# First weight tile fetched ahead of the attention's loads, and the tails' bias copied by DMA

## The chip, the cores and the metric

The program runs on one core of a Trainium2 chip. Five engines of that core matter here: TensorE (PE in the profile), VectorE (DVE), ScalarE (ACT), GpSimd (POOL) and SyncE (SP), whose queue issues every transfer of this kernel. The metric is device time in microseconds (us) of one execution; the median of three runs counts.

## The reference

What is computed, cut to its shape:

```python
# 1. attention, 4 batches x 8 heads, 576 positions, head dim 64, window 128
scores = where(mask, scale * q @ k.T + bias, -1e9); x = softmax(scores) @ v      # x: 2304 x 512
# 2. first layer pair
h = x @ w_in; g = relu(h) ** 2; x = g @ w_out                                    # 512 -> 2048 -> 512, float64 weights
# 3. eight experts, all on all tokens
P = exp(x @ w_gate - max); 8 times: rows and columns of P normalised
out = sum over e of P[:, e] * (relu(x @ w1[e]) @ w2[e])                          # 512 -> 1024 -> 512
```

The weights of step 2 arrive as float64, as pairs of 32-bit words. The kernel turns each into a high and a low fp32r part itself, and every large product is made of three matmuls (high x high, high x low, low x high).

## The kernel before

The work is staged. Attention and the first layer pair run interleaved over the first 600 us or so; the experts follow in an order that is written out by hand and lies outside the change. In the first part the order on each engine is made by a scheduler, from the code's order and its own estimate of when operands are ready. So a statement moved in the code can move instructions of every engine.

Four things matter at the start:

- **Attention units.** A unit is one batch, one pair of heads and one part of the sequence (the first 384 positions, or the rest). `attention_load` loads q and k, two transfers each, `attention_qk` turns them with PE (tiles `tp_k`, `tp_q`) and evicts them (`kf` on ACT, `qwhole` half on ACT and half on DVE). `attention_scores` makes a block of scores in `sc`: a matmul of the identity with `bias`, then two of q with k; DVE takes the minimum (`m`), ACT the exponential (`s`), DVE normalises. `attention_weights` turns `s` with PE (`pt`) and ACT copies it to `p`; `attention_values` multiplies with `v` into `xo`, which becomes the columns `xh`, `xl` of x.
- **Position bias.** DVE builds `bias` in eight instructions (line 150), and POOL masks each twice (lines 151, 155). `tails_ready` copies parts of it into `tbias` for the last 64 positions: eight ACT casts (line 183).
- **Weight tiles.** `fetch(i)` loads tile i (512 KB) into one of three buffers `u`; even tiles are of w_in, odd ones of w_out. `narrow` converts a tile: two ACT passes (lines 458, 460), four DVE passes (461, 462, 465, 469, the last one shown as CUSTOM_DVE_ANT_0 in the trace and as ISA in the order), an ACT rounding to the high part (471) and a DVE difference for the low part (472). The result is `a` (w_in) or `b` (w_out), stored to `d_in` or `d_out` for later chunks of tokens (line 499).
- **First layer.** Chunk 0 of x is the first 384 tokens, hence four attention units. Its first matmul, `h` (lines 119 to 121), needs all of that chunk and the first `a`.

In the code `load(0)` and `load(1)` (the q and k of the first two units) stand at line 443, far ahead of `fetch(0)` and `fetch(1)` at line 681, and the SP queue issues them in that order. A transfer whose condition isn't met holds everything behind it on that queue.

Of the kernel before, what the change touches and what calls it, by code (L numbers as in the profile page):

```python
# [23 lines left out]
def raw(ap):  # L24

    return ap.bitcast(F32)
# [3 lines left out]
def attention_moe_moe2(  # L30
# [12 lines left out]
    nc = tc.nc  # L43
    P = 128
# [7 lines left out]
    TAIL = S - FULL * P  # L52
# [95 lines left out]
    bias = ap.tile([P, H, 2 * P], F32R, name="bias")  # L148
# [10 lines left out]
    tbias = ap.tile([P, NPAIR, P + TAIL], F32R, name="tbias")  # L159
# [17 lines left out]
    def tails_ready():  # L177

        for i in range(SETS):
            nc.gpsimd.memset(qtail[i], 0.0)  # L180
        for hp in range(NPAIR):
            for j in range(2):
                nc.scalar.copy(
                    tbias[j * TAIL : (j + 1) * TAIL, hp, :], raw(bias[0:TAIL, 2 * hp + j, : P + TAIL])
                )

    def attention_load(n, b, hp, rest):

        h0 = 2 * hp
        t = {"rest": rest, "alone": b == 0 and not rest, "whole": n < WHOLE_UNITS}  # L190
        for nm, src in (("k", k), ("q", q)):
            r = t[nm] = ap.tile([P, 3, 2, D], F32, name=f"{nm}raw", tag=f"{nm}raw", bufs=2)
            r0 = 0 if not rest else EARLY - (0 if nm == "q" else P)
            r1 = FULL * P if rest else EARLY
            for j in range(2):
                nc.sync.dma_start(
                    r[:, : (r1 - r0) // P, j, :], src[b, h0 + j, r0:r1, :].rearrange("(t p) d -> p t d", p=P)
                )
            if rest:
                nc.sync.dma_start(  # L200
                    r[:TAIL, (r1 - r0) // P], src[b, h0 : h0 + 2, r1:, :].rearrange("j p d -> p j d")
                )
        return t
# [185 lines left out]
    def load(n):  # L389
        if n < len(units):  # L390
            ts[n] = attention_load(n, *units[n])
# [33 lines left out]
    def advance(n):  # L425
        for kind, m, i in steps[done[0] : n]:
            b, hp, rest = units[m]
            if kind == "q":
                if m == NPAIR:
                    tails_ready()  # L430
                attention_qk(m, ts[m])
                ts[m]["p"] = None
            elif kind == "s":
                attention_scores(hp, ts[m], i)
                if i in (1, FULL):
                    attention_v(m, ts[m])
                    load(m + 2)
            else:
                attention_weights(ts[m], i)
                attention_values(b, hp, ts[m], i)  # L440
        done[0] = max(done[0], n)

    load(0)
    load(1)


    NF1 = FF // P
    d_in = [dram.tile([P, 2, DM], F32, name=f"d_in{f}") for f in range(NF1)]
# [3 lines left out]
    def narrow(src, hi, lo):  # L452

        low, high = src[:, :, 0], src[:, :, 1]
        t = [cv.tile([P, DM], U32, name=f"cv{i}", tag=f"cv{i}", bufs=2) for i in range(4)]

        mag = t[0].bitcast(F32)
        nc.scalar.activation(mag, high.bitcast(F32), AF.Abs)

        nc.scalar.activation(t[3], low, AF.Copy, scale=2.0 ** -29)  # L460
        nc.vector.tensor_scalar(mag, mag, F64_SMALL, F64_LARGE, op0=ALU.max, op1=ALU.min)
        nc.vector.tensor_scalar(
            t[1], t[0], 3, 0x3FFFFFF8, op0=ALU.logical_shift_left, op1=ALU.bitwise_and
        )
        nc.vector.scalar_tensor_tensor(
            t[2], high, 0xC0000000, t[1], op0=ALU.bitwise_and, op1=ALU.bitwise_or
        )

        nc.vector.tensor_add(t[1], t[2], t[3])
        w = t[1].bitcast(F32)  # L470
        nc.scalar.activation(hi, w, AF.Copy)
        nc.vector.tensor_sub(lo, w, raw(hi))
# [3 lines left out]
    def fetch(i):  # L476

        if i < 2 * NF1:
            f, nm = divmod(i, 2)
            fs = slice(f * P, (f + 1) * P)  # L480
            words[i] = cv.tile([P, DM, 2], U32, name="u", tag="u", bufs=3)
            uv = words[i].rearrange("p c w -> p (c w)")
            if nm == 0:
                nc.sync.dma_start(
                    uv.rearrange("p (k f) -> p k f", k=NK),
                    w_in[:, fs].bitcast(U32).rearrange("(k p) f -> p k f", p=P),
                )
            else:
                nc.sync.dma_start(uv, w_out[fs, :].bitcast(U32))

    def moe1_load(c, f):
        out = []
        for j, (nm, dr, nb) in enumerate((("a", d_in[f], 3), ("b", d_out[f], 4))):
            hl = mp.tile([P, 2, DM], F32R, name=nm, tag=nm, bufs=nb)
            if c == 0:
                i = 2 * f + j
                fetch(i + 2)
                narrow(words.pop(i), hl[:, 0], hl[:, 1])
                nc.sync.dma_start(dr, raw(hl))
            else:  # L500
                nc.sync.dma_start(raw(hl), dr)
            hl = [hl[:, 0], hl[:, 1]]
            out.append([x.rearrange("p (k f) -> p k f", k=NK) if nm == "a" else x for x in hl])
        return out
# [174 lines left out]
    pending = []  # L679
    turns = [(c, f) for c in range(NCH) for f in range(NF1)]  # L680
    fetch(0)
    fetch(1)
    ahead = [moe1_load(0, 0), moe1_load(0, 1)]
    loaded = [2]
    for c in range(NCH):
# [16 lines left out]
        for f in range(NF1):  # L702
# [6 lines left out]
            hp, tag = (ps_mm, "mm") if c < NCH - 1 else (ps_at, "at")  # L709
# [574 lines left out]
```

## Time and profile before

| | us |
|---|---|
| median of 3 runs (2118.63 to 2123.6) | 2118.92 |
| profiled execution, its own time | 2118.78 |
| its span (first to last instruction) | 2117.0 |
| PE busy in the span | 2052.1 (97%) |
| DVE busy | 1430.3 (68%) |
| ACT busy | 958.4 (45%) |

The device time holds 1.78 us beside the span. A busy PE is not a PE at its peak, since matmuls are pipelined and their ends are modelled. The line of the page that cuts the span into 40 slices (53 us each) shows where PE is not busy: in the first slice, and a little in the third and fourth.

### The profile page before, as it was taken

To read this page: it belongs to the slowest core of one execution; us is meant where nothing else is said; L and a number is where in the kernel's file an instruction comes from. 1 tells how busy PE (TensorE), PEld (TensorE's weight loads), DVE (VectorE), ACT (ScalarE), POOL (GpSimd) and SP (SyncE) were. 2 spreads that over 40 slices of the span, in tenths; PEclk is the share of its full clock that TensorE was granted. 3 is DMA by queue.
4 is the path that set the end of the run, shared out by engine and by line. 5 is a ranking of instruction groups with operands and counts; after the bars stand their busy time and mean duration, and the time that the engine had idled before them with its cause. 6 is when DMAs were issued, how large, how long until landed. Compare 5 with 4: busy or idle time off the path is not lost.

```text
span 2117.0 us, 31449 instructions
## 1 busy us (share of the span) xinstructions
PE 2052.1 (97%) x11056; PEld 1859.8 (88%) x11056; DVE 1430.3 (68%) x2396; ACT 958.4 (45%) x1902; POOL 1032.7 (49%) x665
## 2 busy tenths in 40 slices
PE   6999999999998899999999999999999999999998
PEld 4877777777897787899998999999999999999998
DVE  7886444432327888877778676777768676777766
ACT  7775444433334444444444534444445534444343
POOL 1112212122437777888887444455456444455452
PEclk9999999999999999999999999999999999999999
DMA  7686756555667877887888977777887878777773
GB/s 213 227 253 209 230 154 178 158 181 171 210 202 265 294 264 282 307 319 288 309 313 296 319 264 260 256 253 254 266 264 260 271 264 259 256 250 258 264 262 125
DMA packets 281981, 525.43 MB, mean 248 GB/s; under 512 B 85840, under 2 KB 130016, under 8 KB 277728
## 3 DMA queue, kind: packets, MB, share of 16 engines
q1 hardware_dynamic: 281824, 523.42, 73.5%
q8 instruction: 89, 1.46, 0.3%
q14 instruction: 68, 0.56, 0.1%
HBM read 379.60 MB, written 143.73 MB: 247 GB/s over the span
## 4 chain that ended last, share of the span: by engine, by line
PE 59%; DVE 9%; ACT 2%; issue 2%; DMA 1%; POOL 1%; SPq 0%; ACTq 0%; DVEq 0%; POOLq 0%
PE y L120 9%; PE y L121 9%; PE y L119 9%; PE g L119 9%; PE g L121 9%; PE g L120 9%; DVE rl L954 1%; DVE o L922 1%; ACT rh L953 1%; DMA d_w<-w2a 1%; DVE o L920 1%; DVE s L644 1%; DVE s L642 1%; PE acc L120 1%; PE acc L121 1%
## 5 line engine op out<-in xcount | busy, mean ns | idle before, releaser
L1104 POOL TENSOR_TENSOR rb<-R,rb 128x768 fp32r<-128x768 f32 x95 | 212.7, 2239 | 334.6 <-ACT rb L1099 306.2
L1135 DVE TENSOR_TENSOR a<-y,a 128x384 f32<-128x384 f32 x434 | 239.7, 553 | 180.1 <-PE y L121 178.2
L1104 POOL TENSOR_TENSOR rt<-R,rt 128x768 fp32r<-128x768 f32 x125 | 238.9, 1924 | 146.1 <-issue 61.7
L111 POOL TENSOR_TENSOR gl<-r,gh 128x512 fp32r<-128x512 f32 (+1 forms) x80 | 97.1, 1214 | 397.7 <-ACT gh L110 379.1
L111 POOL TENSOR_TENSOR w2a<-r,w2a 128x1024 fp32r<-128x1024 f32 x64 | 155.4, 2430 | 67.5 <-ACT w2a L110 67.5
L1099 ACT ACTIVATE rt<-R 128x768 fp32r<-128x768 f32 x128 | 107.7, 841 | 148.7 <-DVE R L1086 90.2
L119 PE MATMUL g<-xt,w1o 128*128 128x384 f32 x512 | 172.7, 337 | 0.8 <-ACT u L827 0.6
L121 PE MATMUL g<-xt,w1o 128*128 128x384 f32 x512 | 172.4, 337 | 0.0
L119 PE MATMUL y<-rt,w2o 128*128 128x384 f32 x512 | 172.2, 336 | 0.1
L120 PE MATMUL g<-xt,w1o 128*128 128x384 f32 x512 | 172.2, 336 | 0.0
L121 PE MATMUL y<-rt,w2o 128*128 128x384 f32 x512 | 172.2, 336 | 0.0
L120 PE MATMUL y<-rt,w2o 128*128 128x384 f32 x512 | 172.0, 336 | 0.0
L120 PE MATMUL y<-w2a,rh 128*128 128x512 f32 x384 | 151.0, 393 | 0.2 <-POOL w2a L111 0.2
L119 PE MATMUL y<-w2a,rh 128*128 128x512 f32 x384 | 151.1, 393 | 0.0
L121 PE MATMUL y<-w2a,rl 128*128 128x512 f32 x384 | 150.1, 391 | 0.0
L1081 DVE TENSOR_TENSOR R<-R,pb 128x768 f32<-128x768 f32 x128 | 137.8, 1078 | 5.2 <-ACT R L1194 2.4
L716 DVE SCALAR_TENSOR_TENSOR r<-h,r 128x512 f32<-128x512 f32 (+1 forms) x80 | 50.9, 636 | 128.8 <-ACT r L714 128.7
L119 PE MATMUL y<-rb,w2o 128*128 128x384 f32 x384 | 129.8, 338 | 2.8 <-DVE a L1135 2.1
L120 PE MATMUL y<-rb,w2o 128*128 128x384 f32 x384 | 130.0, 339 | 2.4 <-POOL rb L1104 2.4
L121 PE MATMUL y<-rb,w2o 128*128 128x384 f32 x384 | 129.8, 338 | 0.0
L121 PE MATMUL g<-xb,w1o 128*128 128x384 f32 x384 | 129.1, 336 | 0.0
L119 PE MATMUL g<-xb,w1o 128*128 128x384 f32 x384 | 129.0, 336 | 0.0
(232 smaller groups left out, 5892.1 us busy)
## 6 DMA issues: line engine op xcount, KB each, us to landing
w1o<-d_w SPq DMA_DIRECT2D x448, 256.0 KB, 3.1
w2o<-d_w SPq DMA_DIRECT2D x224, 512.0 KB, 4.0
d_w<-w1a SPq DMA_DIRECT2D x32, 1792.0 KB, 11.6
d_w<-w2a SPq DMA_DIRECT2D x32, 1536.0 KB, 7.9
a<-d_in SPq DMA_DIRECT2D x64, 512.0 KB, 3.6
b<-d_out SPq DMA_DIRECT2D x64, 512.0 KB, 3.6
r<-in_moe_w_dram SPq DMA_DIRECT2D x64, 512.0 KB, 4.3
u<-in_moe_w_in_dram SPq DMA_DIRECT2D x16, 512.0 KB, 5.1
```

Of the source, the lines that this page charges most:

```text
L111: (eng or nc.gpsimd).tensor_sub(lo, src, raw(hi))
L119: nc.tensor.matmul(ps, lhsT=lh, rhs=rh, start=first, stop=False, **kw)
L120: nc.tensor.matmul(ps, lhsT=lh, rhs=rl, start=False, stop=False, **kw)
L121: nc.tensor.matmul(ps, lhsT=ll, rhs=rh, start=False, stop=last, **kw)
L642: nc.vector.tensor_sub(w1s[n][:, 2], w1s[n][:, 1], a11)
L644: nc.vector.tensor_sub(w1s[n][:, 0], a12, w1s[n][:, 2])
L716: nc.vector.scalar_tensor_tensor(g[:, :n], ph[:, :n], 0.0, r[:, :n], op0=ALU.max, op1=ALU.mult)
L920: nc.vector.tensor_add(acc[e][:, i], y, acc[e][:, i])
L1081: nc.vector.tensor_mul(r, r, pb[:, None, :].to_broadcast([P, 2, HALF]))
L1099: nc.scalar.activation(x[:, 0], R[m, f, h], AF.Copy)
L1104: eng.tensor_sub(x[:, 1], R[m, f, h], raw(x[:, 0]))
L1135: nc.vector.tensor_add(acc[dst][:, dt], ps[:, :HALF], acc[dst][:, dt])
```

## The change

Two edits, both in the first stage. `load(0)` and `load(1)` move to the fetches, so that the code's order is fetch, load, fetch, load; and the eight ACT casts of `tails_ready` become eight transfers on SP, of the same bytes from `bias` to `tbias`, read and written as plain fp32.

```diff
         for hp in range(NPAIR):
             for j in range(2):
-                nc.scalar.copy(
-                    tbias[j * TAIL : (j + 1) * TAIL, hp, :], raw(bias[0:TAIL, 2 * hp + j, : P + TAIL])
+                nc.sync.dma_start(
+                    raw(tbias[j * TAIL : (j + 1) * TAIL, hp, :]), raw(bias[0:TAIL, 2 * hp + j, : P + TAIL])
                 )
...
-    load(0)
-    load(1)
-
...
     fetch(0)
+    load(0)
     fetch(1)
+    load(1)
     ahead = [moe1_load(0, 0), moe1_load(0, 1)]
```

Line numbers behind line 443 fall by 3 or 4 in the changed kernel. The scheduler makes a new order out of it. On DVE, at the program's start (`cv` are the passes of `narrow`; the numbers tell tiles apart: 281 to 283 are tile 0, 297 tile 1), before:

```order
L107 TENSOR_TENSOR wgs<-wg,wgs 128x4x8
L143 CAST ident_r<-ident 128x128
L147 CAST rel<-rel_i 128x256
L150 TENSOR_SCALAR bias<-rel 128x256 x8
L461 TENSOR_SCALAR cv_281<-cv_281 128x512
L462 TENSOR_SCALAR cv_282<-cv_281 128x512
L221 TENSOR_SCALAR qwhole_170<-tp_q 64x3x128
L465 SCALAR_TENSOR_TENSOR cv_283<-u,cv_282 128x512
```

and now:

```order
L107 TENSOR_TENSOR wgs<-wg,wgs 128x4x8
L458 TENSOR_SCALAR cv_281<-cv_281 128x512
L459 TENSOR_SCALAR cv_282<-cv_281 128x512
L462 SCALAR_TENSOR_TENSOR cv_283<-u,cv_282 128x512
L466 ISA cv_282<-cv_283,cv_284 128x1024
L469 TENSOR_TENSOR a<-cv_282,a 128x512
L143 CAST ident_r<-ident 128x128
L147 CAST rel<-rel_i 128x256
L150 TENSOR_SCALAR bias<-rel 128x256 x8
L458 TENSOR_SCALAR cv_297<-cv_297 128x512
```

The whole conversion of tile 0 has moved ahead of the eight bias instructions. On DVE where the first two units end (`m_574`, `m_604` are the minima of the next two units' second blocks, `xl0_90` the low part of x from `xo_505`, the second unit's output), before and now:

```order
L299 TENSOR_REDUCE m_548<-sc_546 128x2
L299 TENSOR_REDUCE m_574<-sc_572 128x2
L321 TENSOR_SCALAR s_547<-s_547,z_549 128x128 x2
L299 TENSOR_REDUCE m_604<-sc_602 128x2
L115 TENSOR_TENSOR xl0_90<-xo_505,xh0_89 128x384
```

```order
L321 TENSOR_SCALAR s_547<-s_547,z_549 128x128 x2
L115 TENSOR_TENSOR xl0_90<-xo_505,xh0_89 128x384
L299 TENSOR_REDUCE m_574<-sc_572 128x2
L299 TENSOR_REDUCE m_604<-sc_602 128x2
```

The minima that open the next blocks now stand behind the second unit's output. On SP, where tiles 6 to 9 are fetched and unit 4 has its v loaded, before and now:

```order
L484 DMA u<-in_moe_w_in_dram 128x4x256
L266 DMA v<-in_v_dram 128x3x64 x2
L499 DMA d_in_189<-a 128x1024
L489 DMA u<-in_moe_w_out_dram 128x1024
L499 DMA d_out_211<-b 128x1024
L484 DMA u<-in_moe_w_in_dram 128x4x256
L489 DMA u<-in_moe_w_out_dram 128x1024
L263 DMA v<-in_v_dram 128x2x64
```

```order
L481 DMA u<-in_moe_w_in_dram 128x4x256
L496 DMA d_in_177<-a 128x1024
L486 DMA u<-in_moe_w_out_dram 128x1024
L496 DMA d_out_199<-b 128x1024
L183 DMA tbias<-bias 64x192 x8
L481 DMA u<-in_moe_w_in_dram 128x4x256
L486 DMA u<-in_moe_w_out_dram 128x1024
L496 DMA d_in_178<-a 128x1024
L496 DMA d_out_200<-b 128x1024
L263 DMA v<-in_v_dram 128x2x64
```

Ten transfers have come between the fetch of tile 7 and the first v load of unit 4: the eight copies, and the stores of the fourth `a` and `b`.

## Rows read from the trace of the kernel before

**Rows 1.** The page's 40 slices, busy tenths of PE and DVE.

```profile
PE   6999999999998899999999999999999999999998
DVE  7886444432327888877778676777768676777766
```

**Rows 2.** Windows: us, length, then busy us of PE, PEld, DVE, ACT, POOL, clock.

```profile
0.00:54.00 54.00, 34.42 (x182) 24.00 (x183) 41.40 (x118) 38.56 (x108) 9.24 (x29) 0.91 0.72 212
54.00:120.00 66.00, 64.95 (x382) 56.51 (x383) 58.50 (x138) 49.21 (x128) 11.82 (x13) 1.00 0.72 236
120.00:180.00 60.00, 53.42 (x296) 40.86 (x295) 54.09 (x133) 42.50 (x110) 6.87 (x7) 1.00 0.77 237
```

**Rows 3.** Timeline of the start: start us, us, engine, line, instruction [idle before].

```profile
1.23 1.03 SPq L196 DMA_DIRECT2D kraw<-in_k_dram  x2
...
3.02 0.22 DVE L143 CAST ident_r<-ident 128x128 fp32r<-128x128 f32 x1
...
3.47 2.93 DVE L150 TENSOR_SCALAR bias<-rel 128x256 fp32r<-128x256 f32 x8
...
5.49 0.49 SPq L484 DMA_DIRECT2D u<-in_moe_w_in_dram  x1
...
10.14 0.66 ACT L458 ACTIVATE cv<-u 128x512 f32<-128x512 f32 x1 [4.02 <-DMA u<-in_moe_w_in_dram]
...
10.83 0.43 DVE L461 TENSOR_SCALAR cv<-cv 128x512 f32<-128x512 f32 x1 [4.44 <-ACT cv L458]
```

**Rows 4.** Groups by line, first 60 us: busy us, mean ns | idle before.

```profile
L465 DVE SCALAR_TENSOR_TENSOR cv<-u,cv 128x512 uint32<-128x512 uint32 x9 | 6.6, 735 | 0.1
L469 DVE CUSTOM_DVE_ANT_0 cv<-cv,cv 128x1024 uint16<-128x1024 uint16 x8 | 5.5, 685 | 0.1
L461 DVE TENSOR_SCALAR cv<-cv 128x512 f32<-128x512 f32 x10 | 4.2, 420 | 5.2 <-ACT cv L458 5.2
L462 DVE TENSOR_SCALAR cv<-cv 128x512 uint32<-128x512 uint32 x9 | 3.8, 421 | 0.1
L183 ACT CAST tbias<-bias 64x192 fp32r<-64x192 f32 x8 | 2.8, 346 | 0.1
...
L471 ACT ACTIVATE a<-cv 128x512 fp32r<-128x512 f32 x4 | 2.5, 624 | 0.0
```

**Rows 5.** Timeline, DVE near 22 and 28 us.

```profile
22.05 0.69 DVE L472 TENSOR_TENSOR a<-cv,a 128x512 fp32r<-128x512 f32 x1 [1.62 <-ACT a L471]
...
27.92 0.61 DVE L321 TENSOR_SCALAR s<-s,z 128x256 f32<-128x256 f32 x2
```

**Rows 6.** Timeline from 40 us to the first layer's first matmul.

```profile
40.98 0.59 SPq L484 DMA_DIRECT2D u<-in_moe_w_in_dram  x1
...
42.14 0.47 ACT L314 ACTIVATE s<-sc,m 128x256 f32<-128x256 f32 x1 [0.63 <-DVE m L299]
...
42.60 0.48 ACT L114 ACTIVATE xh<-xo 128x384 fp32r<-128x384 f32 x1
...
45.31 0.67 ACT L458 ACTIVATE cv<-u 128x512 f32<-128x512 f32 x1 [0.38 <-DMA u<-in_moe_w_in_dram]
...
53.84 0.45 PE L119 MATMUL h<-xh,a 128*128 128x384 f32 x1
```

**Rows 7.** Timeline from 51 us: unit 4's loads, the fourth `a`, their uses.

```profile
51.51 0.38 SPq L263 DMA_DIRECT2D v<-in_v_dram  x1
...
57.30 0.36 PE L289 MATMUL sc<-tbias,ident_r 128*128 128x192 f32 x1
...
58.64 0.69 DVE L472 TENSOR_TENSOR a<-cv,a 128x512 fp32r<-128x512 f32 x1
...
60.25 0.80 SPq L200 DMA_DIRECT2D qraw<-in_q_dram  x1
...
69.55 0.47 PE L227 MATMUL tp<-ident,qraw 128*128 128x128 f32 x2
```

**Rows 8.** Transfers issued in the first 60 us: KB each, median us to landing.

```profile
qraw<-in_q_dram SPq DMA_DIRECT2D x8, 32.0 KB, 2.3
```

## Prediction

> **What bounds the kernel now.** I read the page's slices first. PE is at nine tenths or more almost everywhere; it is not in the first 53 us, and slightly less in the third and fourth slice [rows 1]. The change touches nothing behind the first stage, so I then cut the stage into windows [rows 2]. Up to 54 us PE is busy 34.42 us: 19.6 us are lost there. From 54 to 120 us it is busy 64.95 of 66 us, hence PE sets the pace. From 120 to 180 us 6.6 us are lost, with DVE busy 54.09 of 60 us; behind that PE is at nine tenths again [rows 1]. So the change can win only what brings the first matmul of the first layer, at 53.84 us [rows 6], forward, or what thins the 6.6 us later.
>
> The timeline of the start says what the 19.6 us hang on. DVE finishes the bias at 6.40 us (3.47 + 2.93) and then stands still for 4.44 us, since the first weight tile, issued at 5.49 us, is there only at 10.14 us, where ACT begins after 4.02 us of idling [rows 3]. From there to 28 us DVE stands still only once for long, 1.62 us, for an ACT rounding [rows 5]. It is DVE, then, whose queue sets when the first softmax tiles are ready.
>
> **The change, part by part.**
>
> *The tile comes earlier.* It is issued at 1.23 us instead of 5.49 us. With the same 4.65 us to landing (10.14 - 5.49) it is there at 5.88 us, and DVE starts 0.69 us behind (10.83 - 10.14), at 6.57 us [rows 3]. The time to landing is the uncertain part: the old transfer shared the engines with two more tiles, the new one with small q and k loads only. I keep 4.65 us; 1 us either way is my bound, and it shifts DVE's start by as much.
> The Trainium skill (DMA: Bandwidth & Descriptors, Anatomy of one DMA) fits a transfer issued by GpSimd as about 2.0 us fixed plus its bytes over 436 GB/s, an estimate of 3.2 us for 512 KB. The row has 4.65 us, so the measurement decides; by the page DVE would start 1.45 us earlier, and the forecast would be 2116.9.
>
> *DVE does the whole conversion before the bias.* That is the price in the new order. On DVE tile 0 takes 0.42 + 0.42 + 0.735 + 0.685 us, then waits 0.62 us for the ACT rounding [rows 4] and ends with 0.69 us [rows 5]: 3.57 us, to 10.14 us. Then come the identity, the positions and the bias, 3.38 us (3.02 to 6.40) [rows 3]: the bias is done at 13.52 us, 7.1 us later than before. POOL's masks follow the bias and move along. This delays nothing that decides: the minima on DVE stand behind the bias and four conversion passes anyway.
>
> *DVE up to 28 us.* Before, from 10.83 to 28.53 us DVE got through the third score block's normalisation, 17.70 us [rows 3, 5]. Of that 1.62 us was idle; 2.95 us was tile 0, already done now (0.42 + 0.42 + 0.735 + 0.685 + 0.69); and 0.42 us is a pass of tile 4 that now comes later. 12.71 us are left: 13.52 + 12.71 = 26.23 us. With 0.5 us of waiting for an ACT rounding I take 26.7 us, 1.8 us ahead.
>
> *The casts.* Eight of 346 ns, 2.8 us [rows 4], leave ACT between 13 and 20 us. ACT has that time free in the new order, because it waits for DVE's minima; I count them at nothing of their own. If ACT set the pace they would be worth up to 2.8 us. The copies land well before use: on SP they follow the store of the third `b`, near 44.5 us; with 0.52 us an issue (1.03 us for two [rows 3]) they are out near 48.7 us and, with the 2.3 us of a small transfer [rows 8], landed near 51 us, against a first use at 57.30 us [rows 7]. That cover is 6 us.
>
> *From 28 to 54 us.* Walking the new order with the old durations, the lead of 1.8 us holds up to the second unit's output and is then lost on ACT. The minima of the next blocks stand behind that output on DVE, so the exponentials that began at 42.14 us begin near 43.2 us. From there to the first matmul it was 11.70 us (42.14 to 53.84) [rows 6]. Two of ACT's instructions on that stretch stand elsewhere now, a conversion pass of 0.67 us and an eviction of 0.48 us [rows 6], and its 0.38 us of waiting for tile 6 goes if the tile is there: 10.2 us are left, which ends at 53.4 us. Whether the tile is there is close: its fetch of tile 6 was issued at 40.98 us and landed 4.33 us later (45.31) [rows 6]. Now v loads and q loads stand ahead of it, and it goes out near 42.5 us, lands at 46.8 us and is wanted by ACT near 47.5 us. Each microsecond beyond that would be lost in full. I take 53.4 us, 0.4 us ahead.
>
> *After 54 us.* The same matmuls, and PE paces them up to 120 us, so the 0.4 us pass through. DVE has 1.1 us more of conversion before it (a pass of 0.685 and one of 0.42 us are now behind the first matmul), against 7.5 us of idling from 54 to 120 us [rows 2]: nothing. Between 120 and 180 us the instructions shuffle a little. Nothing in the trace tells the sign; half of the 6.6 us, 3.3 us, is my bound both ways.
>
> *Sum.* 2118.78 (the profiled execution: span 2117.0 and 1.78 around it) less 0.4 = 2118.4 us. The median of the runs is 0.14 us above that execution, so nothing is added. Bounds: landing of the tile 1 us, shuffling 3.3 us, the casts 2.8 us for gains only: 2112 to 2122.5.
>
> **The rivals.**
>
> *Faster (2112).* The lead at 28 us (1.8 us) and the casts (2.8 us) both reach the first matmul, and a third of the 6.6 us goes: 6.8 us, 2112.0. For it: 19.6 us lie open at the start, and the transfer that DVE and ACT waited for comes 4.3 us sooner. Against it: the delay of the bias takes most of this back on the same queue, and ACT's path from 42 us holds no cast.
>
> *Slower (2127).* The SP queue is late for unit 4. Its v was issued at 51.51 us and its last q at 60.25 us, and PE turned that q at 69.55 us [rows 7]. Now ten more transfers stand ahead, two of them stores that wait for DVE: the fourth `a` was done at 59.33 us (58.64 + 0.69) [rows 7]. With the stores out at 60.1 us and ten loads at 0.52 us an issue [rows 3], the last q goes out near 65.3 us and is there 2.3 us later [rows 8], at 67.6 us: 1.9 us to spare. It decides from the point where that `a` slips by more than 1.9 us. At a slip of 3.9 us PE waits 2 us, and the next three units, queued behind the next stores, do the same: 8 us, 2126.8. Against it: that `a` needs only tiles fetched by 43 us.
> The Trainium skill (DMA: Bandwidth & Descriptors, Anatomy of one DMA) says that DMA engines don't wait on semaphores, the issuing sequencer does before it dispatches; the copies and stores then hold SP as this rival has it.
>
> *No effect of the first edit (2118.8).* The scheduler gives all of the lead back, and 54 us is met to the tenth. By time this is the forecast; only the trace would tell.
>
> **How the numbers follow.** Some 0.3%, 6.4 us, is what a measurement of this kernel can tell from no change, and it is larger than every single term above. The forecast with its own range of 2114 to 2122, together with the no-effect case, gets 0.80; the faster rival 0.12; the slower one 0.08. The range of 2112.5 to 2123.5 leaves out the far sides of both. Faster than 2112.5 gets 0.11, slower than 2125.3 gets 0.08, the rest 0.81.
>
> **What would show it.** In the changed kernel's timeline: ACT's first pass on tile 0 near 5.9 us, DVE's bias from about 10.5 to 13.5 us, the third block's normalisation near 26 to 27 us, tile 6 landed before ACT asks for it, and the first matmul of the first layer within 1 us of 53.4 us. In the windows PE should again be busy over 64 of 66 us behind it. The prediction is wrong if that matmul comes over 3 us from 53.84 us, if ACT waits for tile 6 with the copies of `p` behind it, if PE waits for a q or v load near 67 to 70 us, or if the idle time between 120 and 180 us changes by more than 3.3 us.

## The result, and the profile after

The changed kernel is slower: 2133.8 us (median of five runs, 2129.02 to 2134.99) against 2119.57 us (five runs, 2118.63 to 2123.6). The ratio is 1.0059 with an interval of 1.0048 to 1.007. The forecast was 2118.4 us in a range of 2112.5 to 2123.5, with 8 chances in 100 for slower. The profiled execution took 2131.24 us, with a span of 2129.4 us, 12.4 us longer than before.

First the page's slices, busy tenths in 40 equal parts of the span, which answer to [rows 1]:

```profile
PE   6989999999998999999999999999999999999998
DVE  7887444432317788887778666777668666777766
```

Only the third slice (106 to 160 us) of PE has dropped. So the windows again, which answer to [rows 2] (length, then busy us of PE, PEld, DVE, ACT, POOL, granted clock), with one of ten microseconds behind them:

```profile
0.00:54.00 54.00, 35.02 (x171) 24.61 (x172) 41.31 (x113) 34.00 (x94) 10.65 (x29) 0.91 0.68 195
54.00:120.00 66.00, 59.72 (x333) 51.08 (x332) 53.81 (x123) 43.16 (x113) 11.54 (x12) 0.97 0.65 209
120.00:180.00 60.00, 52.55 (x281) 40.00 (x279) 51.42 (x119) 40.60 (x104) 6.08 (x6) 0.97 0.76 234
100.00:110.00 10.00, 8.72 (x47) 7.81 (x48) 4.89 (x8) 3.37 (x8) 1.00 (x2) 0.83 0.85 267
```

The counts behind the x say more than the busy time, which grows when the clock falls. Up to 180 us PE has issued 785 matmuls (171 + 333 + 281) against 860 before (182 + 382 + 296). At 0.173 us each, the distance from one 128x384 matmul to the next at the full clock, the 75 that are missing are 13.0 us, about the 12.4 us of the span; this is an estimate, since not all of the 75 have that shape. Eleven of the 75 are missing by 54 us, 49 more between 54 and 120 us, 15 more up to 180 us. DVE too did less from 54 to 120 us, 123 instructions instead of 138: it was not overloaded, work reached it late.

The start went as forecast (timeline: start, length, engine, line, instruction, idle before):

```profile
1.24 0.49 SPq L481 DMA_DIRECT2D u<-in_moe_w_in_dram  x1
...
5.82 0.66 ACT L455 ACTIVATE cv<-u 128x512 f32<-128x512 f32 x1 [2.90 <-DMA u<-in_moe_w_in_dram]
6.51 0.43 DVE L458 TENSOR_SCALAR cv<-cv 128x512 f32<-128x512 f32 x1 [3.37 <-ACT cv L455]
...
9.66 0.69 DVE L469 TENSOR_TENSOR a<-cv,a 128x512 fp32r<-128x512 f32 x1 [0.70 <-ACT a L468]
...
10.72 2.92 DVE L150 TENSOR_SCALAR bias<-rel 128x256 fp32r<-128x256 f32 x8
```

SP's queue did not (start, time that the issue holds SP, count):

```profile
45.45 0.59 SPq L481 DMA_DIRECT2D u<-in_moe_w_in_dram  x1
...
48.44 6.21 SPq L183 DMA_DIRECT2D tbias<-bias  x8
54.70 0.58 SPq L481 DMA_DIRECT2D u<-in_moe_w_in_dram  x1
...
60.21 0.33 SPq L496 DMA_DIRECT2D d_in<-a  x1
61.63 0.33 SPq L496 DMA_DIRECT2D d_out<-b  x1
62.05 0.41 SPq L263 DMA_DIRECT2D v<-in_v_dram  x1
...
68.20 0.63 SPq L200 DMA_DIRECT2D qraw<-in_q_dram  x1
```

The eight copies hold SP for 6.21 us. One issue takes 0.55 us in the median; two took longer (one of them 1.02 us), and some 1.1 us lie between the issues. Behind them tile 8 goes out at 54.70 us (45.45 before), unit 4's first v at 62.05 us (51.51 [rows 7]) and its last q at 68.20 us (60.25 [rows 7]). Where the missing matmuls are felt is later, on PE:

```profile
98.10 0.33 PE L120 MATMUL acc<-gl,b 128*128 128x384 f32 x1
98.27 0.34 PE L121 MATMUL acc<-gh,b 128*128 128x384 f32 x1
98.87 0.44 PE L119 MATMUL acc<-gh,b 128*128 128x384 f32 x1 [0.26 <-ACT gh L110]
...
100.91 0.45 PE L120 MATMUL acc<-gl,b 128*128 128x384 f32 x1 [1.12 <-POOL gl L111]
101.19 0.43 PE L121 MATMUL acc<-gh,b 128*128 128x384 f32 x1
101.42 0.52 PE L119 MATMUL acc<-gh,b 128*128 128x384 f32 x1
101.74 0.52 PE L120 MATMUL acc<-gl,b 128*128 128x384 f32 x1
...
116.43 0.34 PE L121 MATMUL h<-xh,a 128*128 128x384 f32 x1
119.44 0.79 PE L119 MATMUL acc<-gh,b 128*128 128x384 f32 x3 [2.68 <-ACT gh L110]
```

Before, PE waited 0.8 us in all between 54 and 125 us: behind a group of `h` matmuls stood `acc` matmuls whose inputs were ready, or a unit's attention. Now it waits 6.6 us there, 5.1 of them for `gh` and `gl`, the high and low part of g (total us, times, longest us):

```profile
PE acc L119 <- ACT gh L110: 3.3, 3, 2.7
PE acc L120 <- POOL gl L111: 1.8, 2, 1.1
```

That reserve is used up, and PE waits for its own chain from h over r (the squared relu of h) to gh (2.68 us). After the pause at 99 us the matmuls come 0.32 us apart instead of 0.173 for some 4 us. The granted clock of 100 to 110 us is 0.83, so a part of it lies at the lower level, 1.2 GHz; from 120 to 180 us, behind the second pause, it is 0.97. Before, it was 1.00 from 54 to 180 us [rows 2].

One more thing runs out, the lead of the weights. A group of twelve `h` matmuls needs one `a`, whose conversion ends with DVE's difference for the low part. The time from that end to the group's first matmul is the lead of the conversion. In the kernel before it is 38 us at the first group and 9.6 us at the fourth. At the seventh it was 3.5 us (89.12 less 85.60); now PE meets an `a` that is not finished (92.90 less 93.56). Before:

```profile
84.91 0.69 DVE L472 TENSOR_TENSOR a<-cv,a 128x512 fp32r<-128x512 f32 x1
89.12 0.33 PE L119 MATMUL h<-xh,a 128*128 128x384 f32 x1
```

and now:

```profile
92.87 0.69 DVE L469 TENSOR_TENSOR a<-cv,a 128x512 fp32r<-128x512 f32 x1
92.90 0.33 PE L119 MATMUL h<-xh,a 128*128 128x384 f32 x1
```

In the kernel before, the lead is gone only at the ninth group, at 103 us. With both edits the lag grows from there on: the seventh group begins 3.8 us later than before, the eleventh 14.2 us, the fourteenth still 14.2 us.

### The profile page after: what moved, and what is told of

It is laid out like the page before. It is cut to its first block, busy times and chain, and to the rows that moved or that the text cites. A ratio compares the mean times of both kernels' runs of the same rounds, so it can differ in the third digit from the quotient of the medians.

```text
span 2129.4 us, 31449 instructions
## 1 busy us (share of the span) xinstructions
PE 2056.7 (97%) x11056; PEld 1862.5 (87%) x11056; DVE 1432.7 (67%) x2396; ACT 955.3 (45%) x1894; POOL 1032.9 (49%) x665
## 4 chain that ended last, share of the span: by engine, by line
PE 60%; DVE 7%; issue 2%; ACT 2%; DMA 1%; POOL 1%; SPq 0%; ACTq 0%; DVEq 0%; POOLq 0%
PE y L120 10%; PE y L121 10%; PE y L119 10%; PE g L119 9%; PE g L121 9%; PE g L120 9%; DMA d_w<-w2a 1%; DVE rl L953 1%; ACT rh L952 1%; DVE o L919 1%; DVE s L639 1%; DVE o L921 1%; PE acc L120 1%; PE acc L121 1%; PE acc L119 1%
## 5 line engine op out<-in xcount | busy, mean ns | idle before, releaser
L119 PE MATMUL acc<-gh,b 128*128 128x512 f32 (+1 forms) x320 | 128.1, 402 | 3.3 <-ACT gh L110 3.3
L121 PE MATMUL g<-xb,w1o 128*128 128x384 f32 x384 | 129.0, 336 | 0.0
## 6 DMA issues: line engine op xcount, KB each, us to landing
d_w<-w1a SPq DMA_DIRECT2D x32, 1792.0 KB, 11.4
```

The lines of the kernel that those rows point to most:

```text
L119: nc.tensor.matmul(ps, lhsT=lh, rhs=rh, start=first, stop=False, **kw)
L121: nc.tensor.matmul(ps, lhsT=ll, rhs=rh, start=False, stop=last, **kw)
```

## The experiments

Theory Q, formed from these rows: SP is held by the copies while a stage with no slack waits for what stands behind them. Rivals: the early start of edit 1 costs it (theory E); DMAs as such, or the scheduler's new order as such (theory S), cost it. All ratios are to the kernel before on the same chip. "Edit 1" is the moved fetch, "edit 2" the copies by DMA. Three columns of the table come from the traces: how long copies held SP between 43 and 55 us, from the first issue to the end of the last; DVE's instructions from 54 to 120 us (138 before); and the lead of the conversion at the seventh group of `h` matmuls (3.5 us before).

| run | SP held, us | DVE | lead, us | ratio (95% interval) |
|---|---|---|---|---|
| both edits | 6.21 | 123 | -0.7 | 1.0059 (1.0048 to 1.0070) |
| e1_fetch_only | 0 | 134 | 2.9 | 1.0012 (1.0004 to 1.0021) |
| e4_late_second | 0 | 136 | 3.5 | 1.0015 (1.0006 to 1.0024) |
| e2_dma_only | 6.45 | 123 | -0.7 | 1.0042 (1.0030 to 1.0055) |
| f7_extra8 | 6.88 | 124 | -1.2 | 1.0053 (1.0040 to 1.0066) |
| f8_no_casts | 0 | 136 | 4.4 | 1.0001 (0.9992 to 1.0010) |
| f2_two_only | 2.39 | 134 | 2.9 | 0.9997 (0.9989 to 1.0006) |
| f3_two_early | 0 | 132 | 2.0 | 1.0010 (1.0001 to 1.0019) |
| f1_two_both | 1.65 | 132 | 0.8 | 1.0028 (1.0018 to 1.0038) |
| i1_spread | 4.03 | 126 | 1.3 | 1.0021 (1.0012 to 1.0029) |
| h1_defer | 0 | 141 | 3.3 | 1.0005 (0.9997 to 1.0014) |
| h2_dma_defer | 5.43 | 126 | 1.3 | 1.0042 (1.0030 to 1.0055) |
| h4_after_defer | 7.17 | 124 | -0.7 | 1.0067 (1.0055 to 1.0080) |
| e3_pool_queue | 0 | 133 | 2.9 | 1.0026 (1.0016 to 1.0035) |
| e2_act_queue | 0 | 135 | 4.3 | 0.9998 (0.9989 to 1.0006) |
| e3_act_queue | 0 | 135 | 2.9 | 1.0008 (1.0000 to 1.0017) |
| i3_before_u4 | 0 | 141 | 9.6 | 1.0013 (1.0004 to 1.0021) |
| i2_e2_u4 | 6.74 | 133 | 7.8 | 1.0030 (1.0020 to 1.0040) |
| i4_after_u4 | 5.86 | 131 | 7.6 | 1.0060 (1.0048 to 1.0072) |

**One edit at a time.** e1_fetch_only puts ScalarE's copies back:

```diff
-                nc.sync.dma_start(raw(tbias[...]), raw(bias[...]))
+                nc.scalar.copy(tbias[...], raw(bias[...]))
```

> Edit 1 alone: tile 0 is fetched ahead of the attention's loads, ScalarE copies the tails' position bias. Theory Q (the loss is on SP's queue: the eight copies held it for 6.21 us from 48.44, and two stores stood ahead of unit 4's v, so that v went out at 62.05 instead of 51.51): without the copies v of unit 4 goes out within 3 us of before's 51.51, the first 120 us lose at most 3 us, 2116 to 2123 us against 2119.6. Theory E (the early start: VectorE's passes from 13.6 to 18.3 ran 0.61 instead of 0.42 us beside GpSimd's masks, the score blocks and the tile-6 fetch slipped 1.7 us by the first h): the loss stays, 2129 us or more. Theory S (any reordering by the scheduler may cost this much): no number, but a loss here would have other waits than those of the changed kernel.

e2_dma_only keeps the loads and fetches of before and has only the DMA copies.

> Edit 2 alone: the loads and the first fetches as before, the eight tail copies on SP's queue. Here too the order puts the copies and the stores of tiles 4 and 5 ahead of unit 4's v. Theory Q: v of unit 4 goes out near 60 to 62 us, its k and q near 63 to 68, and the lag of the gated stage at 132 us is 8 to 14 us: 2127 to 2134 us. Theory E: the start is before's own, so the time is within 3 us of 2119.6.

e4_late_second is e1 with another order of the first requests:

```diff
-    fetch(0); load(0); fetch(1); load(1)
+    fetch(0); load(0); load(1); fetch(1)
```

> Edit 1 with the second tile's fetch left behind the second unit's loads (fetch 0, load 0, load 1, fetch 1), copies on ScalarE. Tells how much of edit 1's effect is the second tile standing ahead of the second unit's k and q. Theory Q: within 3 us of before, as edit 1 alone. Theory E: as edit 1 alone, 2129 us or more, since tile 0's conversion and GpSimd's masks meet here too.

Edit 2 alone costs 0.42%, 8.9 us by 2118.6; edit 1 alone 0.12%, 2.5 us, and 0.15% in the other order of the requests. The sum of the two edits, 11.4 us, is close to the 12.5 us of both (0.59%). Theory E falls as the main cause. In e2_dma_only tile 8 went out at 51.07 us and unit 4's v at 58.86 (60 to 62 were expected); with edit 1 alone they are at 47.1 and 52.06 us.

**The hold without the rest.** f7_extra8 is the kernel before, with eight more copies into a tile that nobody reads:

```diff
                 nc.scalar.copy(tbias[...], raw(bias[...]))
+        for hp in range(NPAIR):
+            for j in range(2):
+                nc.sync.dma_start(raw(tscr[...]), raw(bias[...]))
```

> The kernel before, its ScalarE copies of the tails' bias kept, plus the same eight copies by SP into a scratch tile that nobody reads. Nothing waits for these copies and nothing is taken away; only SP's queue and the order that the scheduler makes around it change, and that order is the one of edit 2 alone (stores of tiles 4 and 5 ahead of unit 4's v). Theory Q (SP's queue and what its order does): as slow as edit 2 alone, 2124 to 2130 us against before's 2118.6. Theory T (the tail scores wait for a late tbias): no loss, within 2 us of before.

f8_no_casts clears the tile instead of copying:

```diff
-                nc.scalar.copy(tbias[...], raw(bias[...]))
+        nc.gpsimd.memset(raw(tbias), 0.0)
```

> The kernel before without any copy of the tails' position bias: GpSimd clears that tile instead, so the tails' scores miss their position bias. It prices the eight casts alone. The prediction (casts worth nothing, since ScalarE waits for VectorE there): within 2 us of before's 2118.6. If ScalarE sets the pace between 13 and 20 us: 2 to 3 us faster, 2116 us.

Nothing was taken away in f7_extra8 and nobody waits for the copies, and still 0.53% are lost. SP's queue, and then PE, of that run:

```profile
44.67 6.88 SPq L189 DMA_DIRECT2D tscr<-bias  x8
51.61 0.59 SPq L490 DMA_DIRECT2D u<-in_moe_w_in_dram  x1
...
59.41 0.39 SPq L269 DMA_DIRECT2D v<-in_v_dram  x1
```
```profile
110.45 0.34 PE L121 MATMUL h<-xh,a 128*128 128x384 f32 x1
113.47 0.79 PE L119 MATMUL acc<-gh,b 128*128 128x384 f32 x3 [2.68 <-ACT gh L110]
```

The same wait of 2.68 us as with both edits, without any edit. Here, too, the lag comes late: the seventh group of `h` begins 0.2 us earlier than before, the eleventh 8.2 us later, the fourteenth still 8.2 us. A late `tbias` is excluded as the cause. The casts are worth nothing (f8_no_casts, 1.0001), as the prediction had it: there was nothing to win by removing them.

**Smaller holds.** f2_two_only and f1_two_both move the same bytes in two transfers, with edit 2 alone and with both; f3_two_early asks for the two ahead of the first stage; i1_spread asks for each pair's two copies with its own unit (the theory W of its expectation: tile 8, late behind the copies, is what costs).

```diff
-        for hp in range(NPAIR):
-            for j in range(2):
-                nc.sync.dma_start(raw(tbias[j * TAIL : (j + 1) * TAIL, hp, :]), ...)
+        for j in range(2):
+            nc.sync.dma_start(raw(tbias[j * TAIL : (j + 1) * TAIL, :, :]), raw(bias[0:TAIL, j::2, : P + TAIL]))
```

> Edit 2 alone with the eight copies merged into two transfers of the same bytes (one for each half of the partitions), still on SP at the same place. SP is held for two issues, some 1.6 us by 0.78 us each, instead of 6.2. The order puts one store of tile 5 inside unit 4's four v loads instead of two stores ahead of them. Theory Q: the loss shrinks from 8.3 us to 1 to 4 us, 2119.5 to 2122.5. If the bytes in the DMA engines cost it and not the issues: the loss stays, 2127 us.

> Both edits with the copies merged into two transfers, stores where they were. By the sum of the runs so far, edit 1 alone costs 2.6 us and two transfers nothing: 2121 to 2124 us. If edit 1's later start and the two transfers add up to a new gap on TensorE: 2127 us or more.

> Edit 2 alone, two transfers, asked for ahead of the first stage, so that they stand where SP waits for a free weight buffer anyway (8.8 to 13.1 us in the kernel before) and where the bias is ready. Theory Q: unit 4's v goes out within 2 us of 51.51 us, time within 2 us of before, 2116.6 to 2120.6. If any transfer of these bytes next to the first weight tiles costs (as with the copies on GpSimd's queue, where tile 5 landed 6.9 us after its issue): 2 to 3 us slower, 2121 us.

> Edit 2 alone, the eight copies spread over the units that need them: by the order four of them stand ahead of tile 8's fetch, the others later, two by two. Theory W: tile 8 goes out 2 to 3 us late instead of 5.6, and half of the 8.3 us or less is lost, 2119 to 2123 us. Were it the number of issues on SP as such, 2125 us or more.

SP's queue in f2_two_only:

```profile
44.34 2.39 SPq L182 DMA_DIRECT2D tbias<-bias  x2
46.77 1.44 SPq L483 DMA_DIRECT2D u<-in_moe_w_in_dram  x1
...
50.13 0.38 SPq L262 DMA_DIRECT2D v<-in_v_dram  x1
```

A hold of 2.4 us costs nothing with edit 2 alone, one of 4 us 0.21%, those of 5.4 to 6.9 us 0.42 to 0.53%. (i2_e2_u4, below, does not fit: 6.74 us cost 0.30% there.) f2_two_only moves the same bytes from the same place, so it is the eight issues, with the order made around them, and not the bytes. f3_two_early, in a place where SP was idle, is barely clear of nothing (0.10%). f1_two_both is at 0.28%, 3.4 us above edit 1 alone: beside edit 1 even the small hold is felt.

**Which load behind the copies?** h1_defer issues each tile's stores one turn later, ahead of the next fetch, so that none of them waits for DVE ahead of unit 4's v; h2_dma_defer is edit 2 alone with the same, h4_after_defer both edits.

```diff
     def moe1_load(c, f):
         out = []
+        while late:
+            dr, hl = late.pop(0)
+            nc.sync.dma_start(dr, raw(hl))
...
-                nc.sync.dma_start(dr, raw(hl))
+                late.append((dr, hl))
```

> The kernel before with one thing moved: the stores of a tile's converted weights are issued one turn later, ahead of the next tile's fetch instead of behind the own conversion, so that no store that still waits for VectorE stands in front of unit 4's v, k and q on SP. It is the control for the next run. If the stores cost nothing where they stood: within 2 us of before's 2119; if SP was late for the attention already: up to 3 us faster.

> Edit 2 alone with eight copies on SP, and the same deferred stores: the queue is held as long as in edit 2 alone (6 us), but no store waits ahead of unit 4's v. Theory Q1 (the hold of the eight issues is what costs): v of unit 4 goes out near 52 to 54 us, some 2 to 3 us late, and still 5 us or more are lost against the control. Theory Q2 (the stores of tiles 4 and 5, which the order puts ahead of v once the copies are there, wait for VectorE until 58.4 and hold v): v near 52 to 54 us, and the loss against the control is at most 3 us.

> Both edits with the deferred stores. Theory Q2: of the 12.5 us that both edits cost, some 8 to 9 go; what is left is edit 1's 2 to 3 us, 2120 to 2123 us. Theory Q1: 2127 us or more.

SP's queue in h2_dma_defer:

```profile
43.72 5.43 SPq L183 DMA_DIRECT2D tbias<-bias  x8
...
50.30 0.78 SPq L484 DMA_DIRECT2D u<-in_moe_w_in_dram  x1
...
52.53 0.46 SPq L263 DMA_DIRECT2D v<-in_v_dram  x1
...
58.51 1.12 SPq L200 DMA_DIRECT2D qraw<-in_q_dram  x1
```

v is now 1 us late and the last q is earlier than before, and still 0.37% (1.0042 over 1.0005) are lost against the control. My second version of the theory, that the stores ahead of v do the harm, falls. What is late here is tile 8, by 4.85 us. So I tried that next, with a fourth buffer for raw tiles and fetches one tile further ahead, which puts tile 8 ahead of the copies (theory W: the late tile 8 costs it; theory P: the order around the copies does): i3_before_u4 is the control, i2_e2_u4 edit 2 alone, i4_after_u4 both edits.

```diff
-            words[i] = cv.tile([P, DM, 2], U32, name="u", tag="u", bufs=3)
+            words[i] = cv.tile([P, DM, 2], U32, name="u", tag="u", bufs=4)
...
-                fetch(i + 2)
+                fetch(i + 3)
...
+    fetch(2)
     ahead = [moe1_load(0, 0), moe1_load(0, 1)]
```

> Control for the next run: the kernel before with a fourth buffer for the raw weight tiles and each fetch one tile further ahead. If the tile pipe had no slack anywhere before: some us faster than 2119; if its slack was enough: within 3 us of 2119.

> Edit 2 alone, eight copies on SP, with the fourth buffer: tile 8's fetch now stands ahead of the copies, so the 6 us of SP's hold fall on tiles that are wanted later. Theory W: against the control i3 at most 3 us are lost, no wait of TensorE over 2 us for gh between 100 and 125 us. Theory P: 6 us or more are lost against the control, as the order around the copies is changed here too.

> Both edits with the fourth buffer. Theory W: of the 12.5 us some 8 go, 2119 to 2125 us, edit 1's own 2.6 us staying. Theory P: 2127 us or more.

Inconclusive. The control itself is slower (0.13%). In i2_e2_u4 tile 8 was out at 41.6 us and the loss against the control is down to 0.17%, some 3.5 us and between the two theories, but v was late again (58.17 us), and PE waits 2.2 us for gh all the same. In i4_after_u4 tile 8 was out at 46.6 us, 1.2 us after before's, and 0.47% are lost against the control. So a late tile 8 is not needed for the loss, any more than a late v. In these three kernels the conversion is further ahead, and the lead at the eighth group tells them apart: 6.0 us in the control, 0.9 and -1.0 us in the other two.

**Off SP's queue.** e3_pool_queue has both edits with the copies issued by GpSimd; e2_act_queue and e3_act_queue have them issued by ScalarE, with edit 2 alone and with both.

```diff
-                nc.sync.dma_start(raw(tbias[...]), raw(bias[...]))
+                nc.scalar.dma_start(raw(tbias[...]), raw(bias[...]))
```

> Both edits, but the eight tail copies are issued by GpSimd into its own queue instead of by SP. SP's order is then that of edit 1 alone. Theory Q: v of unit 4 goes out as in edit 1 alone, and the time is that of edit 1 alone within 2 us (2116 to 2123 us), provided the copies land before the first tail score near 57 us. Theory E: the loss stays, 2129 us or more. If the copies by DMA themselves (their landing, 128 x 4 KB rows through the DMA engines) cost the time, it stays as well, with the first tail score waiting for tbias.

> Edit 2 alone, the eight copies issued by ScalarE into its own queue between 13 and 25 us, one or two at a time among its other work. SP holds no copy, so tile 8 and unit 4's v should go out within 2 us of 45.45 and 51.51 us. If the loss is SP's hold: at most 3 us slower than before's 2119 (ScalarE pays the issues, and the transfers may delay tiles 4 and 5 as on GpSimd's queue). If DMAs as such, or any new order, cost it: 2125 us or more.

> Both edits, the eight copies issued by ScalarE. If the loss is SP's hold: edit 1's own 2.6 us and at most 3 us more, 2120 to 2125 us. Otherwise 2129 us or more.

In e2_act_queue the issues hold ScalarE eight times for about half a microsecond, between 11 and 27 us (two of them, then SP's queue):

```profile
14.74 0.47 ACTq L183 DMA_DIRECT2D tbias<-bias  x1
...
21.45 0.61 ACTq L183 DMA_DIRECT2D tbias<-bias  x1
```
```profile
42.92 1.19 SPq L484 DMA_DIRECT2D u<-in_moe_w_in_dram  x1
...
52.37 0.38 SPq L263 DMA_DIRECT2D v<-in_v_dram  x1
...
60.48 0.80 SPq L200 DMA_DIRECT2D qraw<-in_q_dram  x1
```

Tile 8 goes out 2.5 us earlier than before, v and q within 0.9 us of before, and the loss is gone: 0.9998 where the same transfers through SP made 1.0042, and 1.0008 with both edits instead of 1.0059. So it is not DMAs as such. It is not a changed order as such either: of the 881 matmuls that PE issues up to 185 us in the kernel before, about 670 stand in the same sequence in h1_defer and 785 in e2_dma_only, and h1_defer loses 0.05%. What is left is eight issues on SP near 44 to 55 us, together with the order that the scheduler makes around them. (Queue and time of the issue changed together here.) The Trainium skill (DMA: Bandwidth & Descriptors, Issuing engines are not separate DMA queues) says that issuing from several engines saves only the sequencer's time for the issue, which is usually small beside the transfer. The trace agrees for one copy: 0.55 us (median) of SP for a transfer that lands 3.8 us (median) after its issue. What cost here was the place of eight of them in SP's queue. GpSimd's queue did worse than ScalarE's. Its copies left at 18.82 us, and weight tile 5, issued at 20.37 us beside them, landed 6.9 us later instead of 4.2 us with edit 1 alone; ScalarE idled 2.16 us for it, and the first `h` matmul came at 57.03 us (54.18 with edit 1 alone).

No version beats the kernel before: e2_act_queue and f2_two_only equal it.

## Why the prediction was wrong

Right were the steps up to 25 us. Tile 0 was there at 5.82 us (forecast 5.88), DVE began at 6.51 (6.57), the bias was done at 13.6 (13.52), and the first normalisation came at 23.14 instead of 24.98 us, the lead of 1.8 us. Right too was that the casts are worth nothing.

Wrong, but small: from there to 54 us. The sixth normalisation was done at 27.87 instead of 28.53 us, 0.7 us ahead and not 1.8, and in another order of the blocks. Tile 6 went out at 45.45 us instead of the 42.5 of the forecast, ScalarE took it at 50.27, 2.8 us after the 47.5 at which the prediction would have it, and the first matmul of the first layer came at 55.52 us, 1.7 us after before's 53.84 [rows 6] instead of 0.4 ahead. Not foreseen was that DVE's passes run longer beside GpSimd's masks (last section): three by 0.2 us, one by 0.2 and one by 0.1, 0.9 us together.

The step that failed is the one on the copies: "The copies land well before use ... That cover is 6 us." I asked who waits for the copies, and that answer was right (nobody: f7_extra8). I did not ask who waits for SP behind them. One issue was put at 0.52 us, that of a q or k load, and that was about right (median 0.55 us); but two were longer and gaps lay between them, 6.21 instead of 4.2 us in all. The cost to those behind was left at nothing outside the slower rival, where the runs showed 8.9 us (e2_dma_only), and 0.53% with eight copies that nobody reads (f7_extra8). And "After 54 us. The same matmuls, and PE paces them up to 120 us" took the busy 64.95 of 66 us for slack against late loads. It was the opposite: PE was fed from a reserve of `acc` groups and from the lead of the weights' conversion, and both ran out. The lead was gone at 103 us before, inside the stretch that PE was to pace, and is gone at 93 us now; from there on each of the next eight groups begins within 2 us of the end of its `a`. DVE's 7.5 us of idling could not be used, since what it lacked was input: from 54 to 120 us it was busy 53.81 us instead of 58.50.

The slower rival came nearest, and had 8 chances in 100. Its place was SP's queue, right; its price (8 us, 2126.8) is about edit 2's (8.9 us), by luck, since it was to be paid elsewhere. Its point of decision was wrong: it looked for PE waiting for a late q or v near 67 to 70 us, and no such wait appears; PE waits at 99 and 119 us for gh, and h2_dma_defer loses as much with q and v on time.

Open is why a hold of 6 us costs 8 to 10. Part of it is the clock: 0.83 of full speed for 10 us are 1.7 us, 0.97 for the 60 us behind 120 us 1.8 us more (estimates from the granted clock). Of the rest the runs show that the loss grows with the hold, i2_e2_u4 apart, and that with the copies on SP it comes where the lead of the conversion is gone early. What uses the lead up isn't shown: tile 10, which the sixth group needs, is fetched at 66.2 us in f7_extra8 instead of 61.1, but at 60.8 us in h2_dma_defer, and both have little or no lead left at the seventh group. The scheduler orders PE and DVE anew in each of these kernels, and how much of the loss is its order and how much the real lateness could not be separated, since the two change together. Nor was edit 1's own 2.5 us taken apart.

## What to carry to other kernels

A DMA has two costs: its landing, for those who wait for it, and its issue, for everything behind it in the same queue. When work is moved to a queue, multiply the count by the issue time, and ask of each load behind it what it feeds. Here two merged copies (with edit 2 alone) or eight on ScalarE's queue, earlier, cost nothing where eight on SP cost 0.42%. A stage in which the bottleneck engine is never idle isn't one with cover: here lateness showed tens of microseconds later, as a wait for the engine's own chain. Measure how far ahead of the engine its inputs are made, group by group, and where that lead ends.

## What the runs showed of the hardware

The issue of a copy within SBUF holds a queue about as long as that of a load, half a microsecond, on SP as on ScalarE's queue. The copies with both edits, those of e2_act_queue, and the q loads of the kernel before (count: shortest, median and longest in ns, first and last start in us):

```profile
L183 SPq DMA_DIRECT2D tbias<-bias x8: 462/548/1020, 48.4 to 54.1; - x8
L183 ACTq DMA_DIRECT2D tbias<-bias x8: 468/468/607, 11.5 to 26.1; - x8
L196 SPq DMA_DIRECT2D qraw<-in_q_dram x14: 384/488/1437, 2.3 to 59.8; - x14
```

Single issues can be much longer, of loads as of copies. Eight copies one behind the other held SP for 5.43 to 7.17 us in seven runs, gaps included.

DVE's passes and GpSimd's masks both take longer when they run side by side. With edit 1 the masks run from 11 to 18.5 us beside DVE's conversions. DVE, then GpSimd, in the changed kernel:

```profile
13.57 0.61 DVE L458 TENSOR_SCALAR cv<-cv 128x512 f32<-128x512 f32 x1
...
16.84 0.88 DVE L466 CUSTOM_DVE_ANT_0 cv<-cv,cv 128x1024 uint16<-128x1024 uint16 x1
...
20.61 0.68 DVE L466 CUSTOM_DVE_ANT_0 cv<-cv,cv 128x1024 uint16<-128x1024 uint16 x1
```
```profile
12.65 0.85 POOL L151 TENSOR_SCALAR_AFFINE_SELECT bias<-bias 128x256 fp32r<-128x256 f32 x2
...
15.10 1.38 POOL L155 TENSOR_SCALAR_AFFINE_SELECT bias<-bias 128x256 fp32r<-128x256 f32 x2
```

DVE's first pass takes 0.61 instead of 0.42 us [rows 4], its addition 0.88 instead of 0.68; a pair of masks takes up to 1.38 us instead of 0.75 to 0.85 in the kernel before. The Trainium skill (SBUF — State Buffer, Who interferes with whom) says that the two share a pair of ports, that one instruction holds it to its end, and that a DVE instruction with two SBUF inputs contends with GpSimd's reads. The rows agree that both lose; whether one blocks or both slow down they don't tell.
